# A transformer kernel's opening: ACT loads its table before it issues token tile 1, and the first key products run on tile 0 alone

## The chip, the cores and the metric

The kernel runs on one core of a Trainium2 chip. A core has five engines that run side by side, each through its own list of instructions in order: PE (TensorE: matrix products and transposes), DVE (VectorE), ACT (ScalarE), POOL (GpSimd) and SP (SyncE, which here only issues DMA transfers). They wait for each other through semaphores. The metric is the device time of one execution in microseconds (us), as a median of several runs.

## The reference

Two layers on 2048 tokens of width 1024; each layer is a windowed attention and a feed-forward part, both behind a layer norm and with a residual.

```python
def _A_ref(x, wqkv, wo):          # H = 32 heads of 32, window W = 8, dilation 2
    qkv = (x @ wqkv).reshape(B, S, 3, H, Dh) ...
    idx = pos[:, None] - (jnp.arange(W) * dil)[None, :]     # 8 earlier positions, every second one
    ...
    logits = jnp.where(mask, einsum("bhsd,bhswd->bhsw", q, kg) * scale, -1e9)
    o = einsum("bhsw,bhswd->bhsd", softmax(logits), vg)
    return o... @ wo
def _B_ref(x, w1, b1, w2, b2):    # F = 3584
    h = relu(x @ w1 + b1); return (h * h) @ w2 + b2
x = A_x
for _ in range(2):
    x = x + _A_ref(_layernorm(x), A_wqkv, A_wo)
    x = x + _B_ref(_layernorm(x), B_w1, B_b1, B_w2, B_b2)
```

Inputs and weights are bf16.

## The kernel before, in words

The 2048 tokens are cut into four blocks of 512 per layer, eight units of work (u = 0 to 7) in all. A unit goes through the stages SA (load four token tiles of 128, layer norm, transpose them to a tile xnT with the width of 1024 on the partitions), the projections (`projection`, lines 448 to 491: keys, queries, values, eight chunks of 128 columns each, PE accumulates over eight k-steps of 128, then ACT copies the result out of PSUM), S2 (window products on DVE, softmax, values), SW (output projection) and SF_up and SF_down (feed-forward).

The code doesn't issue the instructions as it runs. Every stage adds operations to a planner (`_Plan`), with an engine, an assumed duration, and the buffers that it reads and writes. `schedule` then plays the plan through with these assumed durations and puts each engine's operations in order by due time. PE's main work (`main=True`) keeps the order in which it was added; each main operation stands behind the one before. `issue_behind(a, b)` says that b may be issued only after a. Two instructions that write the same tile or share a buffer are put in an order by semaphores, whichever was emitted first going first. So a change in the opening can reorder what DVE, ACT and SP do later.

The opening is the function `first_projections` with SA(0):

- `SA` (line 428 on) loads four token tiles x0 to x3. x0, x2 and x3 go out through SP's queue, x1 through ACT's (`load_x`, line 413). Behind x0, SP issues four pieces of the key weights (two k-steps of 128 rows each), x2, x3, then four pieces of the query weights (`w_qkv`, line 347). ACT then loads its function table (line 436).
- PE first multiplies a tile of zeros (`spin`, line 743), eleven products of 512 columns whose result is not used.
- `layer_norm` (line 354 on) does, per tile: two halves of statistics on DVE (line 365), an aggregate on DVE (367), logarithm and exponential on ACT (368, 369), the normalisation on DVE (383), eight transposes on PE into one PSUM tile `pt` (398). For tiles 0 and 1 the transposed tile is copied to xnT in two halves: k-steps 0 to 3 by DVE (401), k-steps 4 to 7 by ACT (402). For tiles 2 and 3 DVE copies it whole (404). Lines 384 to 387 hold tile 0's normalisation back until tile 1's aggregate has been issued.
- Then come the key products of the first 256 tokens (tiles 0 and 1) for five of the eight chunks, step by step through all five chunks: tokens 0 to 127 with the first weight piece, tokens 128 to 255 with the first piece, then all 256 tokens with pieces two, three and four. Between the transposes of tile 0 and tile 1 stands one more product of zeros.
- After that: keys of chunks 5 to 7, tile 2's transposes, queries, tile 3's transposes, the second half of the tokens, and the values.

PSUM has six buffers that `pt`, the projections and most other products share (tag "mm"), so a product also waits until a buffer was copied out.

## Time and profile before

| | |
|---|---|
| median of three runs | 1238.55 us (1237.99 to 1238.65) |
| the profiled execution's own time | 1238.63 us |
| its span (first to last instruction) | 1236.9 us |
| PE busy | 1230.4 us, 99% |
| DVE, ACT, POOL busy | 67%, 45%, 14% |
| mean DMA rate | 206 GB/s |

The span is shorter than the execution's own time by what lies around the instructions. Engine rows in the profile give the start and the length of an instruction or of a run of equal ones; "[1.38 <-DVE xn L383]" says that the engine had been idle for 1.38 us and what ended that. A name with a q (SPq, ACTq) is the engine's sequencer, which issues DMAs and waits. `L398` is line 398 of the kernel before. The changed kernel is three lines shorter from line 387 on (its transposes are L395, its copies L398 and L399, its projections L472).

### The profile page before, as it was taken

The page shows a single profiled execution, that of the slowest core. Times are in us where ns is not written, and L with a number is a line of the kernel's source. Part 1 is how long each engine was busy: PE and PEld are TensorE (multiplying, and loading weights), DVE is VectorE, ACT ScalarE, POOL GpSimd, SP SyncE. Part 2 cuts the span into 40 slices and gives each one's busy share as a digit, 9 for nine tenths or more (in the row PEclk, how much of TensorE's full clock was granted, in tenths as well). Part 3 has the DMA queues.
Part 4 walks back from the last instruction along what each step waited for, and adds up shares of the span by engine and source line. Part 5 has one row for each costly group of instructions (what it writes and reads, how often), then busy time and mean ns, then how long its engine had stood idle before and what let it go on. Part 6 is the DMA issues. An engine that isn't in the chain of part 4 may idle for free.

```text
span 1236.9 us, 15608 instructions
## 1 busy us (share of the span) xinstructions
PE 1230.4 (99%) x5907; PEld 637.6 (52%) x5907; DVE 825.2 (67%) x1233; ACT 560.3 (45%) x1031; POOL 170.7 (14%) x200
## 2 busy tenths in 40 slices
PE   8999999999999999999999999999999999999998
PEld 7665444554455544555445554455544564444444
DVE  6899893698906979079770888609895199972001
ACT  5626920479104691048901578016770146612720
POOL 1351000040500100005050020000505011000000
PEclk9999999999999999999999999999999999999999
DMA  6858857688567985689755997548965596569441
GB/s 230 241 192 227 240 191 231 181 237 224 174 213 199 243 246 161 207 213 276 226 188 170 259 278 205 176 151 278 273 198 174 166 260 195 164 190 235 154 136 51
DMA packets 258277, 255.15 MB, mean 206 GB/s; under 512 B 70458, under 2 KB 221210, under 8 KB 258202
## 3 DMA queue, kind: packets, MB, share of 16 engines
q1 hardware_dynamic: 258058, 253.90, 69.5%
q8 instruction: 46, 0.75, 0.3%
q10 hardware_dynamic: 144, 0.26, 0.1%
q14 instruction: 29, 0.24, 0.1%
HBM read 209.98 MB, written 12.58 MB: 180 GB/s over the span
## 4 chain that ended last, share of the span: by engine, by line
PE 99%; DMA 0%; DVE 0%; issue 0%
PE py L715 31%; PE ph L690 31%; PE pq L475 27%; PE py L665 9%; PE lg L514 0%; DMA xt<-in_A_x_dram 0%; PE pt L398 0%; DVE stats L365 0%; PE junk L743 0%; DVE xo L725 0%; DVE xn L383 0%; DVE mv L367 0%; PE b1ps L329 0%
## 5 line engine op out<-in xcount | busy, mean ns | idle before, releaser
L715 PE MATMUL py<-wt,r2t 128*128 128x512 bf16 (+1 forms) x1820 | 388.3, 376 | 0.0
L690 PE MATMUL ph<-xnT,wt 128*128 128x512 bf16 x1792 | 388.1, 379 | 0.0
L475 PE MATMUL pq<-xnT,wt 128*128 128x512 bf16 (+2 forms) x1674 | 336.9, 362 | 0.0
L715 PEld LDWEIGHTS <-r2t 128*128 128x128 bf16 x1820 | 177.6, 98 | 209.4
L475 PEld LDWEIGHTS <-wt 128*128 128x128 bf16 x1674 | 229.9, 144 | 105.4 <-issue 3.4
L690 PEld LDWEIGHTS <-wt 128*128 128x128 bf16 x1792 | 174.9, 98 | 211.6
L484 ACT CAST kT<-pq 128x512 bf16<-128x512 f32 (+1 forms) x72 | 38.5, 540 | 352.7 <-PE pq L475 351.4
L693 ACT ACTIVATE r<-ph,b1T 128x512 bf16<-128x512 f32 x224 | 151.8, 678 | 51.0 <-PE ph L690 50.9
L502 DVE TENSOR_TENSOR P<-qT,kT 128x2048 bf16<-128x2048 bf16 x128 | 154.1, 1235 | 8.8 <-ACT qT L484 5.5
L615 DVE TENSOR_TENSOR pr<-pb,vT 128x2048 bf16<-128x2048 bf16 x128 | 153.3, 1234 | 7.6 <-DMA pb<-p 7.6
L695 ACT ACTIVATE r2t<-r 128x512 bf16<-128x512 bf16 x224 | 139.8, 629 | 5.7
L725 DVE TENSOR_TENSOR xo<-py,xm 128x512 bf16<-128x512 f32 (+1 forms) x33 | 22.3, 675 | 157.4 <-PE py L715 154.9
L618 DVE TENSOR_TENSOR pr<-pr 128x1024 bf16<-128x1024 bf16 (+1 forms) x256 | 126.7, 552 | 0.0
L519 DVE TENSOR_TENSOR P<-P 128x2048 bf16<-128x2048 bf16 x98 | 118.9, 1220 | 1.2
L665 PE MATMUL py<-wt,oT 128*128 128x512 bf16 x512 | 111.8, 379 | 0.0
L668 DVE TENSOR_TENSOR xm<-py,xt 128x512 f32<-128x512 f32 x64 | 43.0, 681 | 94.4 <-PE py L665 93.8
L491 POOL COPY khalo<-kT 128x7 bf16<-128x7 bf16 x64 | 20.2, 320 | 477.1 <-ACT kT L484 477.1
L491 POOL COPY vhalo<-vT 128x7 bf16<-128x7 bf16 x64 | 51.2, 809 | 243.7 <-ACT vT L484 243.2
L465 POOL COPY vT<-vhalo 128x7 bf16<-128x7 bf16 x32 | 67.0, 2143 | 125.5 <-DVE pr L615 125.3
L665 PEld LDWEIGHTS <-oT 128*128 128x128 bf16 x512 | 50.0, 98 | 60.2
L729 DVE TENSOR_TENSOR xm<-py,xm 128x512 f32<-128x512 f32 x32 | 21.5, 688 | 81.9 <-PE py L715 81.8
L368 ACT ACTIVATE lnv<-mv,eps 128x1 f32<-128x1 f32 x36 | 10.5, 292 | 95.0 <-DVE mv L367 95.0
(61 smaller groups left out, 547.6 us busy)
## 6 DMA issues: line engine op xcount, KB each, us to landing
wt<-in_B_w_dram SPq DMA_DIRECT2D x56, 1024.0 KB, 6.9
wt<-in_B_w_dram SPq DMA_DIRECT2D x64, 896.0 KB, 5.0
wt<-in_A_wqkv_dram SPq DMA_DIRECT2D x44, 1024.0 KB, 6.2
wt<-in_A_wo_dram SPq DMA_DIRECT2D x16, 1024.0 KB, 5.9
xt<-xs SPq DMA_DIRECT2D x32, 512.0 KB, 4.2
pb<-p SPq DMA_DIRECT2D x64, 128.0 KB, 4.5
xs<-xm SPq DMA_DIRECT2D x32, 256.0 KB, 3.4
xt<-in_A_x_dram SPq DMA_DIRECT2D x31, 256.0 KB, 4.0
```

Source lines behind the costliest of these rows:

```text
L465: add("POOL", 0.2, lambda: nc.gpsimd.tensor_copy(dst.t[:, 0:off], prev.t[:, c0, :]), r=[(prev, c0)], w=[(dst, 0)])
L475: nc.tensor.matmul(pq.t[:, a - t0:b - t0], w[:, kd % 4, c0:D:8], xnT.t[:, kd, a:b], start=first and kd == k0, stop=last and kd == k1 - 1, ...
L491: add("POOL", 0.2, lambda: nc.gpsimd.tensor_copy(halo.t[:, c0, :], dst.t[:, BLK:BLK + HALO]), r=[(dst, 2)], w=[(halo, c0)])
L502: st["dve"].append(add("DVE", 1.14, lambda: nc.vector.tensor_tensor(P.t[:], q.t[:, hb * HB:(hb + 1) * HB].rearrange("q (g t) -> q g t", g= ...
L519: self.state[u]["dve"].append(self.plan.add("DVE", 1.14, lambda: self.nc.vector.tensor_tensor(a.t[:], a.t[:], b.t[:], ALU.add), r=[b], w=[a]))
L615: dve.append(add("DVE", 1.14, lambda v=v, pr=pr: nc.vector.tensor_tensor(pr.t[:], pb.t[:], _win_ap(v.t, HALO + hb * HB, HB, groups=G), ALU ...
L618: dve.append(add("DVE", d, lambda pr=pr, k=k: nc.vector.tensor_tensor(pr.t[:, :, 0:k, :], pr.t[:, :, 0:k, :], pr.t[:, :, k:2 * k, :], ALU. ...
L665: nc.tensor.matmul(py.t[:], st["o", c].t[:, tl * 128:(tl + 1) * 128], st["wo"][db].t[:, c, :], start=(c == 0), stop=(c == self.NCH - 1))
L690: nc.tensor.matmul(ph.t[:], wt.t[:, kd, cc * 128:(cc + 1) * 128], xnT.t[:, kd, :], start=(kd == 0), stop=(kd == self.KD - 1))
L693: add("ACT", 0.58, lambda ph=ph, r=r, f=f: nc.scalar.activation(out=r.t[:], in_=ph.t[:], func=ACTF.Relu, bias=self.b1T[:, f:f + 1], scale= ...
L695: add("ACT", 0.54, lambda r=r, r2t=r2t: nc.scalar.activation(out=r2t.t[:], in_=r.t[:], func=ACTF.Square), r=[r], w=[r2t])
L715: nc.tensor.matmul(py.t[:], r2[kf].t[:, tl * 128:(tl + 1) * 128], wt.t[:, kf - k0, c0:c1], start=(kf == 0), stop=(kf == KF - 1))
```

## The change

Three places are touched. In `SA`, ACT's table load comes first and the issue of x1 behind it; before, it was the other way round. In `layer_norm`, tile 0's normalisation is no longer held behind tile 1's aggregate. In `first_projections`, the key products on tiles 0 and 1 are cut and ordered anew: three short products of zeros (128 columns) follow tile 0's transposes, then tile 0 alone goes through the first two weight pieces for five chunks (twenty products of 128 columns), then come tile 1's transposes, then tile 1 through the same two pieces (twenty more), and then both tiles together through pieces three and four. Before, the second piece was multiplied with both tiles at once. `spin` takes the number of columns, and its assumed duration follows from it.

```diff
-            aggr = add("DVE", 0.12, lambda: nc.vector.bn_aggr(...), r=[stats], w=[mv])
+            add("DVE", 0.12, lambda: nc.vector.bn_aggr(...), r=[stats], w=[mv])
...
-            norm = add("DVE", 0.45, lambda: nc.vector.tensor_scalar(out=xn.t[:], ...), r=[xt, mv, rstd], w=[xn])
-            if tl == 1:
-                plan.issue_behind(aggr, self.norm0)
-            self.norm0 = norm
+            add("DVE", 0.45, lambda: nc.vector.tensor_scalar(out=xn.t[:], ...), r=[xt, mv, rstd], w=[xn])
...
-            self.plan.issue_behind(x1, table)
+            self.plan.issue_behind(table, x1)
...
-    def spin(self, n):
+    def spin(self, n, cols=BLK):
...
-            add("PE", 0.427 if n > 4 else 0.3, lambda: nc.tensor.matmul(self.junk.t[:], self.zeros.t[:, 0:128], self.zeros.t[:], start=True, stop=True),
+            add("PE", cols * 8.3e-4, lambda: nc.tensor.matmul(self.junk.t[:, :cols], self.zeros.t[:, 0:128], self.zeros.t[:, :cols], start=True, stop=True),
                 r=[self.zeros], w=[self.junk], main=True)
...
-        for n, norm in ((11, norms[0]), (1, norms[1])):
-            self.spin(n)
-            norm()
+        self.spin(11)
+        norms[0]()
+        self.spin(3, 128)
...
-        early = first("wk", [(0, 128, 0, 2), (128, HB, 0, 2)] + pairs[1:])
-        for _ in range(5):
+        early = first("wk", [(t, t + 128, k, k + 2) for t in (0, 128) for k in (0, 2)] + pairs[2:])
+        for i in range(6):
+            if i == 2:
+                norms[1]()
             for p in early:
                 next(p, None)
```

In a step `(a, b, k0, k1)`, a to b are the tokens and k0 to k1 the k-steps.

More of the change, by code (lines that the diff above doesn't have):

```diff
@@ L366, in layer_norm @@
                     r=[(xt, h)], w=[(stats, h)])
-            aggr = add("DVE", 0.12, lambda: nc.vector.bn_aggr(out=mv.t[:], in_=stats.t[:].rearrange("p (n f) -> p n f", n=2)), r=[stats], w=[mv])
+            add("DVE", 0.12, lambda: nc.vector.bn_aggr(out=mv.t[:], in_=stats.t[:].rearrange("p (n f) -> p n f", n=2)), r=[stats], w=[mv])
             add("ACT", 0.2, lambda: nc.scalar.activation(out=lnv.t[:], in_=mv.t[:, 1:2], func=ACTF.Ln, bias=self.eps[:], scale=1.0), r=[mv], w=[lnv])
@@ L382, in layer_norm @@
         if pe_transpose:
-            norm = add("DVE", 0.45, lambda: nc.vector.tensor_scalar(out=xn.t[:], in0=src(), scalar1=mv.t[:, 0:1], scalar2=rstd.t[:],
+            add("DVE", 0.45, lambda: nc.vector.tensor_scalar(out=xn.t[:], in0=src(), scalar1=mv.t[:, 0:1], scalar2=rstd.t[:],
                                                             op0=ALU.subtract, op1=ALU.mult), r=[xt, mv, rstd], w=[xn])
-            if tl == 1:
-                plan.issue_behind(aggr, self.norm0)
-            self.norm0 = norm
         else:
```

## The prediction

> **What bounds the kernel now.** I read the page's head and chain first, then PE's waits, then the order of time of the first 28 us.

> The page, its head and the shares of the chain that ended last:

> ```profile
> span 1236.9 us, 15608 instructions
> PE 1230.4 (99%) x5907; PEld 637.6 (52%) x5907; DVE 825.2 (67%) x1233; ACT 560.3 (45%) x1031; POOL 170.7 (14%) x200
> PE 99%; DMA 0%; DVE 0%; issue 0%
> ```

> PE's waits over the whole span (who waited for whom; us, times, longest):

> ```profile
> PE junk L743 <- DVE zeros L741: 1.7, 1, 1.7
> PE pt L398 <- DVE xn L383: 1.4, 1, 1.4
> ```

> PE is the bound and waits only twice, both in the opening. After 7.99 us it never waits again, so whatever moves the opening moves the end one for one, and new PE idle time is added in full. The change lies in the opening alone; here it is in order of time (start, us, engine, line):

> ```profile
> 0.81 0.39 ACTq L413 DMA_DIRECT2D xt<-in_A_x_dram  x1
> 0.81 0.41 SPq L413 DMA_DIRECT2D xt<-in_A_x_dram  x1
> 1.23 1.28 ACT L436 ACT_TABLE_LOAD   x1 [1.23 <-PEq L832]
> 1.73 4.88 PE L743 MATMUL junk<-zeros 128*128 128x512 bf16 x11 [1.73 <-DVE zeros L741]
> 4.73 1.88 DVE L365 BATCH_NORM_STATS2 stats<-xt 128x6 f32<-128x512 bf16 x3 [2.74 <-DMA xt<-in_A_x_dram]
> 6.75 0.29 ACT L368 ACTIVATE lnv<-mv,eps 128x1 f32<-128x1 f32 x1 [4.24 <-DVE mv L367]
> 7.31 0.21 DVE L367 BATCH_NORM_AGGREGATE mv<-stats 128x2 f32<-128x12 f32 x1
> 7.43 0.49 DVE L383 TENSOR_SCALAR xn<-xt,mv,rstd 128x1024 bf16<-128x1024 bf16 x1
> 7.99 1.03 PE L398 MATMUL pt<-ident,xn 128*128 128x128 bf16 x8 [1.38 <-DVE xn L383]
> 9.06 0.42 DVE L401 COPY xnT<-pt 128x512 bf16<-128x512 bf16 x1 [0.40 <-PE pt L398]
> 9.52 0.58 ACT L402 COPY xnT<-pt 128x512 bf16<-128x512 bf16 x1 [1.44 <-DVE xnT L401]
> 10.93 1.88 DVE L365 BATCH_NORM_STATS2 stats<-xt 128x6 f32<-128x512 bf16 x3 [0.16 <-DMA xt<-in_A_x_dram]
> 17.55 0.61 PE L398 MATMUL pt<-ident,xn 128*128 128x128 bf16 x8
> 21.43 1.06 ACT L375 ACTIVATE xn<-xt 128x1024 bf16<-128x1024 bf16 x1 [3.30 <-DMA xt<-in_A_x_dram]
> 22.48 1.79 ACT L484 CAST qT<-pq 128x256 bf16<-128x256 f32 x6
> ```

> Three things are to be seen. Tile 0's normalisation (7.43) stands behind tile 1's aggregate (7.31). Each tile's transposes are copied in two halves, DVE first and ACT behind it, and the first key products need DVE's half only. And PE starts slow: eight transposes take 1.03 us at 7.99 but 0.61 at 17.55, the spins 0.43 each. Taken singly, products of 128 columns start 0.107 us apart up to 10.84 and 0.06 apart from 10.91 on; the trace's clock record begins at 10.85. I call that the release.

> **The change part by part.** Times below are in this execution's span (its own time 1238.63 us, 1.73 above the span; the median shown is 1238.55).

> *The issue of tile 1.* Nothing here shows a DMA issue behind a table load. Bounds: the table doesn't hold ACT's queue of issues, tile 1 goes out at about 0.85 and both tiles land as now (4.71 and 4.52); or it holds it for its 1.28 us, to 2.1. Tile 0 then has the DMA engines alone: they move 390 to 400 GB/s from 3 us on, so without tile 1's 256 KB it lands up to 0.67 us earlier, at 4.04. Tile 1 then lands 3.7 us (its time now) to 4.4 after its issue, 5.8 to 6.5, which DVE needs at about 6.6: hidden. I take the first: ACT's sequencer has a semaphore record at 23.91 in the middle of a CAST that runs until 24.27, so it runs ahead of its engine. On SP, the third query piece instead of the second now waits for tile 1; with keys and tiles 2 and 3 queued until 11.57 that starves nothing.

> *Tile 0 without tile 1 in front.* Statistics 4.73 to 6.02, aggregate 0.03+0.21, Ln 0.03+0.29, Exp 0.03+0.20, normalisation 0.04+0.52, hand-over to PE 0.06: transposes at 7.44 instead of 7.99, **0.55 us gained**.

> *Copies.* In the order that the planner writes for the changed kernel, ACT's half of a tile is copied first and DVE's copy waits for it. Transposes 1.03 + 0.04 + ACT 0.58 + 0.04 + DVE 0.42 + 0.06 = 2.17: the first key products start at 9.61. The three short spins cover 0.32 us (3 x 0.107), so PE sits idle from 8.61 to 9.61. Tile 1's first statistics half, now on DVE ahead of this copy, ends at about 8.0 and is hidden by ACT's copy, until 9.1.

> *Twenty products on tile 0* (five chunks, pieces 0 and 1), 0.107 each while slow: 9.61 to 11.74. Meanwhile tile 1 is normalised behind tile 0's DVE copy (ends 9.55): statistics to 10.15, aggregate, Ln, Exp and normalisation as above, to 11.53. Transposes of tile 1 at 11.74 (11.59 if the clock is up by then).

> *Tile 1's copies are bare.* PE's next work after these transposes is tile 1's own products, so transposes, ACT copy, DVE copy and hand-over lie in a row: 2.17 us, of which PE works 0.85. Now, twenty products of tile 0 and a spin cover that. Slow, tile 1's products start at 13.91; fast (0.61 for 1.03), at 13.34. Tile 2's statistics stand ahead of that DVE copy and wait for a tile landing at 10.9: hidden by 1.9 us.

> *Twenty products on tile 1*: ten products of 256 columns (0.109 each) became twenty of 128 (0.0615 in the ten from 11.03 to 11.65): +0.14. Done at 13.34+1.23 = 14.57 fast, 13.91+2.13 = 16.04 slow. Today the same products are done at 12.75. So **+1.8 us with the release at 10.85**, +3.3 in the slow case, plus half of the time that PE still runs slowly after 16.04.

> *Behind the opening.* ACT now has the next block's square (L376, L377: 0.2 + 1.15 + 0.19) in front of the query copies; it starts when a tile lands at 21.40, and the first copy ends at about 24.35 instead of 22.84. PE needs that bank at 23.70 today. With PE 0.66 us or more late this costs nothing; were PE not late, it would stall here, so no case ends below +0.66. Exp of tile 3 moved behind five key copies, but its transposes (20.19 today) come more than 1.5 us after the normalisation that follows. The opening's later SP queue differs only in which of the waiting transfers goes first (query-half, transposed tiles): PE's reduces and products have 1.5 us or more in hand over what they wait for up to 51 us, and the bound of that part is 0 to +0.3.

> *When is the release?* It decides between 1.8 and more. The row: it came 2.87 us after PE's restart at 7.99, in unbroken work. But the 4.7 us of unbroken spins from 1.73 brought none, so it isn't a count from a restart. A grid of fixed stretches fits: the stretch that ends at 10.85 was busier than the two before it. That allows a length of 3.2 to 3.65 us; at 3.41 the three are 67%, 70% and 84% busy. In the changed kernel (tile 1 issued early) the stretch 7.44 to 10.85 has 1.17 + 1.24 = 71% and 10.85 to 14.26 has 61%, nearest to those without a release; 14.26 to 17.67 is full. So: release at about 17.7, and from 16.04 on half of 1.63 = 0.8 us more. **Sum: 3.3 + 0.8 = +4.1 us.** A count of 2.87 us of unbroken work would run from 9.61 to 12.48, in the middle of the slow transposes' end: +2.4.

> [...]

> **The rivals.**
> 1. *Issued early, release at 10.85 as now*: for it, 71% is little more than the 70% that failed; +1.8, 1240.4.
> 2. *Issued early, release by unbroken work at 12.5*: +2.4, 1241.0; the spins speak against it.
> 3. *The table holds the issue (ending not slower than a measurement can tell).* Tile 0 lands at 4.04, transposes at 6.77; spins and transposes fill 90% of the stretch 4.03 to 7.44 and it releases at 7.44. Then the chain alone counts: 6.77 + 4.15 to tile 1's transposes (7.44 to 11.59 above) + 1.75 for these, fast, with both copies (2.17 - 0.42) + 1.23 = 13.9, **+1.2, 1239.7**. It decides if tile 0 lands before about 4.2 (at 4.2 that stretch is 84% busy). The sequencer record speaks against the hold.
> 4. *The table holds, and no release before 17.7* (tile 0 after 4.2): products on tile 1 done at 15.4, half of 2.3 us slow behind: +3.8, 1242.3.
> 5. *Faster*: the copies run side by side after all and the whole of tile 0's gain is kept. It needs tile 1's bare 1.3 us covered, which no row offers, and the query copies' floor of +0.66 stands against it.

> **How the numbers follow.** Forecast (early issue, late release) 40%, rival 1 15%, 2 12%, 3 18%, 4 10%, 5 and anything unseen 5%. Predicted: 1238.55 + 4.1 = 1242.6 us. Stretch lengths up to 3.65 give releases up to 18.15 and +4.4, with 0.3 behind the opening 1243.3; the low end is rival 3 at its earliest, +1.0, 1239.5. A measurement of this kernel can tell about 0.2%, 2.5 us, from no change, so 1241.0 is the border: the forecast, rival 4 and half of 2 lie above (56, rounded 57%), rivals 1 and 3 and the other half below (40%), 3% is left for faster.

> **What would show it.** Right: transposes at about 7.4; PE idle of 1.0 us ahead of the first L475 and 1.3 ahead of tile 1's, both put down to DVE's copy; that copy waiting for ACT's; no PE wait behind 14 us; a clock record that begins at 17 to 18 us. The table held: ACT's issue at 2.1, first statistics at about 4.1. Wrong altogether: PE waits beyond 20 us, or DVE's copy starting right behind the transposes.

## The result and the profile after

The changed kernel takes **1241.15 us** (1239.75 to 1242.06) where the kernel before took 1238.53 us (1237.89 to 1239.64) on the same chips: a ratio of **1.0019, 95% interval 1.0011 to 1.0026**, 2.6 us slower. That is on the border of what a measurement here can tell from no change. The forecast was 1242.6 us, with a range from 1239.5 to 1243.3.

The profiled execution of the changed kernel took 1239.92 us with a span of 1238.2 us, 1.3 us more than the span of before. PE's waits over the whole span (us in total, times, longest):

```profile
PE pq L472 <- DVE xnT L398: 2.1, 2, 1.1
...
PE pt L395 <- DVE xn L383: 1.1, 2, 0.6
PE ph L687 <- ACT r L690: 0.3, 1, 0.3
```

Before, PE waited once behind its spins. Now it waits four times in the opening: twice for a normalised tile, twice (2.1 us in all) for DVE's half of a copy. A short wait for ACT far behind the opening is new, too. Here is the opening in order of time (start, us, engine, line), first ACT's rows, then DVE's, then PE's:

```profile
0.80 1.28 ACT L433 ACT_TABLE_LOAD   x1 [0.80 <-PEq L831]
0.83 0.40 ACTq L410 DMA_DIRECT2D xt<-in_A_x_dram  x1
...
7.80 0.58 ACT L399 COPY xnT<-pt 128x512 bf16<-128x512 bf16 x1 [1.31 <-PE pt L395]
...
8.42 0.43 DVE L398 COPY xnT<-pt 128x512 bf16<-128x512 bf16 x1 [0.74 <-ACT xnT L399]
...
12.17 0.42 DVE L398 COPY xnT<-pt 128x512 bf16<-128x512 bf16 x1
...
7.13 0.64 PE L395 MATMUL pt<-ident,xn 128*128 128x128 bf16 x8 [0.53 <-DVE xn L383]
...
8.90 1.40 PE L472 MATMUL pq<-xnT,wt 128*128 128x128 bf16 x20 [0.96 <-DVE xnT L398]
10.90 0.62 PE L395 MATMUL pt<-ident,xn 128*128 128x128 bf16 x8 [0.60 <-DVE xn L383]
12.65 0.54 PE L472 MATMUL pq<-xnT,wt 128*128 128x128 bf16 x6 [1.13 <-DVE xnT L398]
```

Tile 0's transposes come 0.86 us earlier than before (7.13 for 7.99). Then the row of ACT's copy, DVE's copy and hand-over stands bare twice: PE is idle for 0.96 us ahead of tile 0's products and for 1.13 us ahead of tile 1's, and in between for 0.60 us, until tile 1 is normalised. Tile 1's twenty products, 0.0615 us each, are done at 12.65 + 1.23 = 13.88 where before had the same work done at 12.75: +1.1. The wait for ACT's `r` adds 0.3; together 1.4, of which 1.3 is seen in the span.

This execution is one of the faster ones. Its clock came up as the transposes began (0.64 us for the eight, not 1.03), and the trace's clock record begins at 7.20. Of the 14 runs, those whose mean granted clock prints as 1.0 took 1239.75 to 1240.36 us, those with 0.998 or 0.999, which by that mean were clocked lower for some time after the first record, 1240.40 to 1242.06. No run of the second group was profiled, so when and how far is not shown. The mean is a rough witness in two ways. Time ahead of the first record counts as full speed: the profile of before prints 1.0 though its products of 128 columns start 0.107 us apart up to 10.84 and 0.06 apart from 10.91 on. And a little half speed at the very end, where PE no longer works, counts as well (before's last 0.6 us).

### The profile page after: what moved, and what is told of

Read it like the earlier page. It is cut to its first block, busy times and chain, and to the rows that moved or that the text cites. A ratio compares the mean times of both kernels' runs of the same rounds, so it can differ in the third digit from the quotient of the medians.

```text
span 1238.2 us, 15524 instructions
## 1 busy us (share of the span) xinstructions
PE 1224.0 (99%) x5808; PEld 637.6 (51%) x5919; DVE 825.3 (67%) x1233; ACT 560.8 (45%) x1031; POOL 171.3 (14%) x200
## 4 chain that ended last, share of the span: by engine, by line
PE 98%; DMA 1%; issue 1%; DVE 0%; ACT 0%; SPq 0%
PE py L712 31%; PE ph L687 30%; PE pq L472 27%; PE py L662 9%; DMA xnT<-xn 1%; PE lg L511 0%; DMA xt<-in_A_x_dram 0%; PE pt L395 0%; DVE stats L365 0%; ACT xnT L399 0%; ACT xn L375 0%; DVE xn L383 0%; DVE xnT L398 0%; ACT lnv L368 0%; ACT r L690 0%
## 5 line engine op out<-in xcount | busy, mean ns | idle before, releaser
L488 POOL COPY vhalo<-vT 128x7 bf16<-128x7 bf16 x64 | 54.1, 854 | 239.8 <-ACT vT L481 239.5
L368 ACT ACTIVATE lnv<-mv,eps 128x1 f32<-128x1 f32 x36 | 10.5, 291 | 97.9 <-DVE mv L367 97.9
```

Of the source, the lines that this page charges most:

```text
L488: add("POOL", 0.2, lambda: nc.gpsimd.tensor_copy(halo.t[:, c0, :], dst.t[:, BLK:BLK + HALO]), r=[(dst, 2)], w=[(halo, c0)])
```

## The experiments

Two theories were set against each other. **Idle theory**: the loss is PE standing bare behind each of the two transpositions, by the order in which the planner puts the copies. **Clock theory**: the loss is the half-speed stretch that this idle time brings. Differences are against the kernel before on the same chip, whose medians were 1238.24 (the first three and the table alone), 1238.67 (the changed kernel again, the hold alone, the table put back, the first version of all together), 1238.45 (the order of tile 1's copy on two kernels, the second version of all together) and 1238.58 us (the order of the query copies). The 95% interval of most of these ratios reaches about 0.0009 to either side, 1.1 us, so smaller differences between two kernels are read from the traces' waits and not from the medians. Line numbers in a run's rows are those of its own kernel.

### DVE's half first

```diff
-                add("DVE", 0.4, lambda: nc.vector.tensor_copy(dst(0, mid), ...), r=[pt], w=[lo])
-                add("ACT", 0.5, lambda: nc.scalar.copy(dst(mid), ...), r=[pt], w=[hi])
+                c0 = add("DVE", 0.4, lambda: nc.vector.tensor_copy(dst(0, mid), ...), r=[pt], w=[lo])
+                c1 = add("ACT", 0.5, lambda: nc.scalar.copy(dst(mid), ...), r=[pt], w=[hi])
+                plan.issue_behind(c0, c1)
```

> The changed kernel, with ACT's half of the copies of tiles 0 and 1 issued behind DVE's half. Copies theory (the loss is that PE waits for DVE's copies, each 0.62 us later because ACT's copy of 0.58 us stands in front of it): PE's idle time ahead of the first key products falls from 1.19 to about 0.5 us, ahead of tile 1's products from 1.35 to about 0.7, and the median falls by 1.2 us to about 1239.9. Clock theory (the loss is a later release of the PE clock): the idle time falls but the median stays within 0.4 us of 1241.15, or follows only where the clock record begins earlier.

Measured: 1239.51 us (1239.07 to 1241.12), +1.27, with a span of 1237.7 us. PE's waits for DVE's copies fell from 2.1 to 1.4 us, all of it at tile 0 (0.3 us left); tile 1's longest is as before:

```profile
PE pq L473 <- DVE xnT L398: 1.4, 2, 1.1
...
PE pq L473 <- ACT qT L482: 0.2, 1, 0.2
```

DVE's rows in order of time show why tile 1's copy is still late:

```profile
10.91 0.69 DVE L365 BATCH_NORM_STATS2 stats<-xt 128x6 f32<-128x512 bf16 x1 [0.66 <-DMA xt<-in_A_x_dram]
11.52 0.41 DVE L398 COPY xnT<-pt 128x512 bf16<-128x512 bf16 x1
```

DVE stands idle for 0.66 us until tile 2 lands, works on its statistics, and copies tile 1 only then: the planner had put these statistics in front of the copy. Tile 1's products come 0.67 us earlier (11.98 for 12.65), and 0.2 us of that is given back to a new wait for a query copy; another 0.2 us goes to the wait for ACT's `r`, which was 0.3 in the changed kernel.

### Tile 1's transposes one step earlier

```diff
-            if i == 2:
+            if i == 1:
                 norms[1]()
```

> The changed kernel with tile 1's transposes one step earlier: ahead of the second weight piece on tile 0 instead of behind it, so ten products of tile 0 (0.62 us) lie over tile 1's copies. Copies theory: PE's idle time ahead of tile 1's products falls from 1.35 to about 0.7 us and the median by 0.6 us, to about 1240.5. Clock theory: the same idle time in all lies in other places, and the median moves by less than 0.3 us.

Measured: 1239.55 us (1239.43 to 1240.03), +1.31, span 1237.7. Half of tile 0's products now cover tile 1's copies: PE has one wait for DVE's copy left (1.0 us, tile 0's) and the same new wait of 0.2 us for a query copy. Each of the two bare idles can be taken away by itself, and each time the span of the one profiled execution is 0.5 us shorter than that of the changed kernel. The medians alone don't show these gains: the changed kernel was not run on this chip, and its own loss was +2.6 in its first runs and +1.37 on another chip (below).

This profiled execution holds a half-speed stretch (9.02 to 12.43; tile 1's transposes take 1.04 us) and yet took 1239.44 us, and the five runs with a mean clock of 0.999 lie among the six with 1.0. So here a half-speed stretch costs nothing that the time shows. A reason that fits, not tested, is that PE would only have waited longer for the query copy.

### The idle filled with products that nobody uses

Nine short products of zeros behind tile 0's transposes instead of three, and ten behind tile 1's.

```diff
-        self.spin(3, 128)
+        self.spin(9, 128)
...
                 norms[1]()
+                self.fill(10)     # products of zeros, 128 columns, into a buffer of their own
```

> The changed kernel with more products of zeros: nine of 128 columns instead of three behind tile 0's transposes, and ten behind tile 1's, where PE is idle today. Clock theory: PE is busy enough everywhere, the clock is released at about 7 us in every execution, the spread of 2.3 us shrinks to under 1 us and the median falls to that of the fastest executions of the changed kernel, about 1240.0. Copies theory: the real products still start when DVE's copies end, so nothing is gained below 1239.9; if the clock plays no part in the spread, the median stays at 1241.1.

Measured: 1239.92 us, +1.68; ten of the eleven runs lie within 1239.77 to 1240.06 and one at 1241.0. The mean clock prints as 1.0 in all of them. The spread of 2.3 us is nearly gone, and the median is no lower than what the changed kernel takes at full clock: with the clock held up, the order of the copies still costs its 1.7 us. The small spread is what the clock theory expected, the floor of 1239.9 what the copies theory expected; the two had forecast nearly the same median, so the median does not part them. One thing weakens this as a test of the clock alone: the later wait for ACT's `r` is absent here as well.

### The changed kernel once more, beside three others

> The changed kernel once more, beside the kernels it is to be compared with. Both theories: 1241.0 +- 0.5 us, +2.6 against before. Idle theory (the loss is PE standing bare behind each of the two transpositions, 1.2 and 1.35 us): the runs whose record shows full clock throughout lie +1.2 to +1.9 above before, and that part stays in every run. Clock theory (the loss is the half-speed stretch that the idle brings in some executions): runs with full clock lie within 0.5 us of before, and only those with a mean clock below 1 lie above.

Measured: 1240.04 us (1239.46 to 1241.62), +1.37, ratio 1.0015 (1.0006 to 1.0023), below the 1241.0 +- 0.5 that both theories expected. The four lowest runs, all at full clock, stay 0.8 to 1.1 us above before's median, and the two other runs at full clock 1.6 and 2.3 us. The clock theory wanted them within 0.5 us: the fixed part is there, with a lower end than the idle theory's +1.2. Its profiled execution (1240.97, full clock from 7.44 on) has the same opening within 0.2 us and yet a span of 1239.2, 1.0 more. The waits, ACT's rows in order of time, and ACT's row of the kernel before show where:

```profile
PE ph L687 <- ACT r L690: 1.2, 1, 1.2
```

```profile
432.96 1.06 ACT L375 ACTIVATE xn<-xt 128x1024 bf16<-128x1024 f32 x1 [8.26 <-DMA xnT<-xn]
...
434.02 0.67 ACT L690 ACTIVATE r<-ph,b1T 128x512 bf16<-128x512 f32 x1
```

```profile
430.31 1.06 ACT L375 ACTIVATE xn<-xt 128x1024 bf16<-128x1024 f32 x1 [6.51 <-DMA xnT<-xn]
```

At 433 us a statistics pass of layer two, which waits for a transfer, stands on ACT ahead of the copies that free PE's buffers. Before, that pass starts at 430.31 and PE does not wait. In the two profiles of the changed kernel it starts at 431.92 and 432.96 and costs 0.3 and 1.2 us. So there is a third term that neither theory had: a place far behind the opening that changes from run to run.

### Single parts of the change

The hold alone taken from the kernel before (table and products as before):

```diff
-            if tl == 1:
-                plan.issue_behind(aggr, self.norm0)
```

> The kernel before with one part of the change alone: the statistics of tile 1 are no longer held behind tile 0's normalisation; table behind tile 1's issue, products in pairs of 256 as before. Idle theory: PE's order and the copies of both tiles are as before, so no bare idle of over 0.7 us behind the transposes; 1238.2 +- 0.5 us. If the hold itself was what kept tile 0's normalisation early, it comes 0.6 us later and the time is 1238.8 us or more. Clock theory: the same work in the same stretches, 1238.2 us.

Measured: 1240.94 us (1240.30 to 1242.83), +2.27. Both theories missed. (The edit takes away the hold of tile 0's normalisation behind tile 1's aggregate; the expectation names it the other way round.) Its PE waits:

```profile
PE py L713 <- DVE xm L727: 1.5, 2, 1.0
PE ph L688 <- DMA xnT<-xn: 1.4, 1, 1.4
PE pq L473 <- ACT qT L482: 0.6, 1, 0.6
```

The opening is fine: no wait for a copy, first key products at 9.36 us, where before has them at 10.09. The loss is 3.5 us of waits at 23, 115, 192 and 194 us. One order less in the opening, and the planner puts later parts in another order; around 104 us, for instance, SP issues a second token tile ahead of two transposes (104.26 against 107.38 and 108.99), where before it came between two (109.11, behind 106.33 and ahead of 110.08). Which of these orders makes which wait was not followed further.

The table alone ahead of tile 1's issue, on the kernel before:

```diff
-            self.plan.issue_behind(x1, table)
+            self.plan.issue_behind(table, x1)
```

> The kernel before with one edit: ACT's table load ahead of the issue of tile 1. Both theories: tile 0 lands about 0.3 us earlier (4.4), because ACT's issue now follows SP's by 0.02 us instead of leading it; tile 0's normalisation is still held behind tile 1's aggregate, so PE starts 0 to 0.1 us earlier and the median stays within 0.4 us of 1238.5. If the table order were what costs the changed kernel its time, it would show +1 us or more here.

Measured: 1241.08 us (1239.30 to 1242.19), +2.84, another miss, and above the +1 us that was set as the sign of the table's order being the cost. DVE's rows in order of time:

```profile
10.96 0.69 DVE L365 BATCH_NORM_STATS2 stats<-xt 128x6 f32<-128x512 bf16 x1 [1.64 <-DMA xt<-in_A_x_dram]
11.57 0.41 DVE L401 COPY xnT<-pt 128x512 bf16<-128x512 bf16 x1
```

Here too tile 1's copy stands behind statistics that wait for tile 2's landing, and PE waits 0.8 us for it. The profiled execution is the fastest of its runs; what puts the others 1.5 us above it is not shown.

The table put back behind the issue, in the changed kernel:

```diff
-            self.plan.issue_behind(table, x1)
+            self.plan.issue_behind(x1, table)
```

> The changed kernel with the table put back behind tile 1's issue. Idle theory: tile 0 lands at about 4.7 us again and its transposes come at 7.9 to 8.0 us instead of 7.13, while the two idles behind the transposes stay at 1.0 to 1.35 us each: 0.3 to 0.9 us above the changed kernel's full-clock runs, 1240.4 to 1241.0 us, median with the clock's share 1241.6. If the table's place only matters through the copies' order (as in the kernel with the table edit alone), the time is that of the changed kernel, 1241.1 us, or below it.

Measured: 1241.20 us (1240.09 to 1242.35), +2.53, and 1.16 above the changed kernel's median on the same chip; lowest run against lowest run it is 0.63, within the idle theory's 0.3 to 0.9. Tile 0's statistics start at 4.76 instead of 4.40 and 4.55, its transposes at 7.95 instead of 7.13 and 7.28. So within the change the table's place is a part that gains, though the same edit alone cost 2.84 us. Not all of the 0.82 us is the landing (0.36): here DVE also works on half of tile 1's statistics ahead of tile 0's aggregate, three halves in a row where the changed kernel has two:

```profile
4.76 1.88 DVE L365 BATCH_NORM_STATS2 stats<-xt 128x6 f32<-128x512 bf16 x3 [2.76 <-DMA xt<-in_A_x_dram]
```

PE's rows show the clock falling in mid-opening:

```profile
7.95 0.67 PE L395 MATMUL pt<-ident,xn 128*128 128x128 bf16 x8 [2.08 <-DVE xn L383]
...
11.84 1.06 PE L395 MATMUL pt<-ident,xn 128*128 128x128 bf16 x8
```

Tile 0's transposes are fast (0.67 us), tile 1's slow (1.06), and the clock record has half speed from 8.39 to 15.21. PE also waits 0.7 us at 117 us for a transposed tile, so this profile does not price the table's place by itself.

### The orders put back, one at a time

The statistics of tiles 2 and 3 behind DVE's copy of tile 1, on top of DVE's half first:

```diff
+                if pe_transpose and tl >= 2:
+                    plan.issue_behind(self.copy1, o)     # o: this half's statistics
...
-                c0 = add("DVE", 0.4, ...
+                c0 = self.copy1 = add("DVE", 0.4, ...
```

> The changed kernel with VectorE's half of the copies first, as measured, and one order more: the statistics of tiles 2 and 3 behind VectorE's copy of tile 1. Theory (that copy stands behind the first statistics of tile 2, which wait for its landing near 10.9 us): PE's bare idle ahead of tile 1's products falls from 1.27 to about 0.65 us, and the query copies are also planned earlier, so the wait for the query copy (0.2 us) goes: 1238.6 +- 0.3 us where the kernel with the copies alone took 1239.5. Rival (the idle is the copy's own latency behind the transposes): still 1.2 us of idle and 1239.5 us.

Measured: 1239.39 us (1239.07 to 1239.90), +0.94. The opening did as the theory said: from PE's last transpose of tile 1 to its first product the starts lie 0.74 us apart, not 1.27. But the time hardly moved, because another wait grew from 0.2 to 0.9 us (PE's waits, then ACT's rows in order of time):

```profile
PE pq L475 <- ACT qT L484: 0.9, 1, 0.9
```

```profile
23.20 1.15 ACT L379 ACTIVATE xn<-xt,nmean 128x1024 bf16<-128x1024 bf16 x1
...
24.34 1.45 ACT L484 CAST qT<-pq 128x256 bf16<-128x256 f32 x5
```

The next block's square stands on ACT ahead of the query copies, and it waits for a token tile that lands at its own time. This is the floor that the prediction priced at +0.66; the fastest run here is 0.62 us above before's median. The next edit takes it away:

```diff
+            if self.qcopy:                               # in layer_norm, next block's first ACT statistics
+                plan.issue_behind(self.qcopy, o)
+                self.qcopy = None
...
+        if (u, nm, c0, half) == (0, "wq", 4, 0):         # the copy of the fifth query chunk
+            self.qcopy = o
```

> The changed kernel with VectorE's copies first, the order edge of tile 1's copy (together measured at 1239.4 us, with a PE wait of 0.9 us for the query copy at 24 us), and the first five query copies of half 0 ahead of the next block's first ACT statistics. Theory (the query copy behind that square takes back what the opening gains): the wait of 0.9 us goes, 1238.3 to 1238.7 us, and the record shows no PE wait beyond 14 us. Rival (the time is set by the half-speed stretches and what follows, the query wait is only seen because PE came early): 1239.2 to 1239.6 us, the 0.9 us reappearing at a later wait or as clock.

Measured: **1238.25 us** (1238.05 to 1239.59), 0.33 below before, ratio 0.9999 (0.9990 to 1.0008). The query wait is gone, and against before on each chip 1.3 us came off. One wait beyond 14 us is left against the expectation, 0.6 us at 432 us for ACT's `r`, the place seen above; that execution took 1239.06. So the change with three orders fixed is as fast as the kernel before: what it lost came of the planner's order, at three places. All eleven runs print a mean clock of 1.0, so this run does not say how much the orders gave by themselves and how much by keeping the clock up.

The order of DVE's copy on the kernel with the table alone:

```diff
 (the table alone, as above)
+                if pe_transpose and tl >= 2:
+                    plan.issue_behind(self.copy1, o)
```

> The kernel before with the table ahead of tile 1's issue, as measured (1241.1 us), and the statistics of tiles 2 and 3 behind VectorE's copy of tile 1. Theory (the table edit lost by the planner's order of that copy, not by the queue): no PE idle behind tile 1's transposes, 1238.0 to 1239.2 us, within 0.5 us of before. Rival (the half-speed stretches are the whole loss, the long idle ahead of the first transposes stays): 1240.5 to 1241.2 us.

Measured: 1244.97 us (1243.47 to 1245.44, five runs), +6.5, the slowest of all and outside both expectations. The idle behind tile 1's transposes is gone, and in its place stand these waits of PE:

```profile
PE py L717 <- DVE xm L731: 2.5, 2, 2.0
...
PE pq L477 <- ACT qT L486: 1.5, 1, 1.5
```

The 2.5 us are lost at 194 and 196 us, for the same buffer as at 192 and 194 us in the kernel without the hold. One order mended, two others disturbed; the half-speed stretch from 7.98 to 11.39 comes on top.

### All of it together

On the changed kernel: DVE's half first, tile 1's transposes one step earlier, the query copies ahead of the next block's statistics, the first half of tile 1's statistics ahead of tile 0's normalisation (where DVE waits for ACT's logarithm and exponential), and 12 and 6 spins for 11 and 3. First without the order of tile 1's copy, then with it. The lines not shown yet (`aggr0` and `norm0` are tile 0's aggregate and normalisation):

```diff
-        self.spin(11)
+        self.spin(12)
...
-        self.spin(3, 128)
+        self.spin(6, 128)
...
+                if pe_transpose and tl == 1 and h == 0:
+                    plan.issue_behind(self.aggr0, o, self.norm0)
```

> The changed kernel with four edits that keep PE covered: VectorE's half of the copies first, tile 1's transposes one step earlier, the first half of tile 1's statistics ahead of tile 0's normalisation, query copies ahead of the next block's first ACT statistics, and 12 and 6 spins for 11 and 3. Idle theory: the two bare idles shrink from 1.2 + 1.35 us to some 0.5 + 0.5 us, and 0.2 us of the wait for the query copy goes: 1.5 to 1.9 us below the changed kernel's full-clock runs, 1237.6 to 1238.6 us, level with before or up to 0.6 us below it, with a spread under 1 us. Clock theory: the stretches are filled above 79%, so the clock stays up, but the order of copies is worth nothing by itself: as the filled kernel, 1239.9 us. Early landing alone (tile 0's transposes 0.86 us earlier than before) would give 1237.4 us if all of it reached the end.

Measured: 1238.79 us, +0.12. Seven runs at full clock lie within 1238.67 to 1238.82; the other four, at a mean clock of 0.998 or 0.999, within 1240.26 to 1240.96. That misses both expectations, 1237.6 to 1238.6 us with a spread under 1 us and 1239.9. That a stretch has to be 79% full for the clock to stay up is shown by no run: with the hold alone it stayed up behind 49% (1.68 us of PE work from 5.01 to 8.42). The profile, one of the seven, has one long wait for DVE's copy left (1.7 us ahead of tile 1's products, with the copy at 11.64 behind tile 2's statistics at 11.03) and none behind the opening. The two groups, 1.5 to 2.2 us apart, go with the mean clock; that the clock alone parts them is not shown, as none of the four was profiled.

> The kernel with the four edits that keep PE covered (1238.8 us, with one bare idle of 1.94 us left ahead of tile 1's products) and the same order edge. Theory: that idle falls to 0.3 us or less, 1237.1 to 1237.6 us in most runs, 1.0 to 1.5 us below before. Rival (the later schedule takes back what the opening gains, or the landing of tiles 2 and 3 is needed sooner): 1238.5 us or more, with PE waits beyond 20 us that the kernel with the four edits has not.

Measured: **1237.00 us** (1236.93 to 1237.12), ratio **0.9989 (0.9980 to 0.9998)**, 1.45 below before. PE's rows in order of time:

```profile
7.27 0.62 PE L402 MATMUL pt<-ident,xn 128*128 128x128 bf16 x8 [1.17 <-DVE xn L390]
...
8.41 0.79 PE L480 MATMUL pq<-xnT,wt 128*128 128x128 bf16 x10 [0.18 <-DVE xnT L405]
9.27 0.62 PE L402 MATMUL pt<-ident,xn 128*128 128x128 bf16 x8
9.72 3.50 PE L480 MATMUL pq<-xnT,wt 128*128 128x128 bf16 x43
```

From 8.41 us on PE does not wait again, the pass at 433 us starts at 427.58, and the mean clock prints as 1.0 in all eleven runs. The change's gain, tile 0's transposes 0.72 us earlier, is now kept. It is not the whole of the 1.45 us: PE is fast here from these transposes on (0.62 us), and in the profile of before its first transposes take 1.03 us and its products are slow until 10.85. The kernel before with its clock up early was not run, so the two shares stay open.

## Why the prediction was right, and where it was wrong

**Slower, inside the range, 1.45 us too high at the point.** The steps in turn:

- *The issue of tile 1.* Right: ACT's issue is at 0.83, beside the table load (0.80 to 2.08). That tile 0 lands as now was wrong to the good side: its statistics start at 4.40, 0.33 earlier, and the 0.55 us gained became 0.86.
- *Copies.* Right in order and in cause: DVE's copy starts at 8.42, put down to ACT's. From transposes to first products it was 8.90 - 7.13 = 1.77 us; the 2.17 was the slow clock's, and without its 0.42 it is 1.75.
- *Tile 1's copies are bare.* Right to the hundredth for the fast case: 12.65 - 10.90 = 1.75 us. But "hidden by 1.9 us" for tile 2's statistics held only for a late tile 1. With these transposes at 10.9, the statistics are the next thing late, as DVE's half first showed; in the changed kernel ACT's copy (11.55 to 12.13) just covers them.
- *Behind the opening.* The floor of the query copies was right: it costs the changed kernel nothing and stops every faster opening, by 0.2 to 0.9 us. The bound of 0 to +0.3 for the rest was looked up to 51 us only; the place at 433 us cost 0.3 and 1.2.
- *When is the release?* This step failed. It took the stretch that ended at 10.85 in one execution of before and laid the changed kernel over the same grid: release at 17.7, with the slow case's 3.3 for 1.8 and the 0.8 behind it. The length of a stretch, 3.41 us, one value out of the 3.2 to 3.65 that before allows, was an estimate; the half-speed stretches of three other kernels last 3.41 us. The phase is not fixed: the record starts at 7.20 and 7.44 in the two profiles of the changed kernel, at 4.52 to 6.75 in ten other kernels. So there is no clock term, only a spread of it: nothing that the mean clock shows in 11 of the changed kernel's 25 runs, and in the slowest some 2 us, the place at 433 us included. With an early release the sum is the chain alone, 13.88 - 12.75 = +1.1. That is rival 3's total, reached without its cause: the table held nothing. One figure on the way was off as well: the 70% for the stretch 4.03 to 7.44 counts the spins at 0.427 us each; the view of stretches has PE busy for 2.58 us there, 76%.

Of its own signs, the idles ahead of the products (0.96 and 1.13 us for 1.0 and 1.3), put down to DVE's copy, and that copy waiting for ACT's came true. The clock record (7.20 for 17 to 18) did not, and the sign for "wrong altogether", a PE wait beyond 20 us, did come, with 0.3 and 1.2 us at 433 us.

That the median lies in the range is in part luck. The forecast's +4.1 us holds 2.3 us for a late release that neither profile of the changed kernel shows. The measured +2.6 is 1.1 us of the chain, 0.3 us or more at 433 us, and a rest in runs of which none was profiled.

The result stands 0.15 us above the border at 1241.0 that was set for "slower", and on another chip the changed kernel's median was 1240.04: which side it falls on hangs on how many of its runs have a mean clock below 1 or lose time at 433 us.

What the prediction had not seen at all is how far single edits reach: the hold alone costs 2.27 us, mostly beyond 20 us, the table alone 2.84. That the whole change is not worse than its parts is a property of this one plan.

## What to carry to other kernels

Where a planner orders the work, an edit in the opening is a new order of all that follows: compare the order of each engine's instructions, look for one that waits for a landing ahead of one that releases PE, and fix those few places with an explicit order. A gain in an opening is kept only if the next engine on the path (here ACT's query copies, which took back 0.2 to 0.9 us) is moved along. Take a clock's phase from no single execution (here the records began at 4.52 to 10.85 us): price it as a spread, or keep PE's idle short (with the idle filled, all eleven runs print a mean clock of 1.0).

## What the runs showed of the hardware

```profile
3.79:7.20 3.41, 2.88 (x8) 0.83 (x7) 2.17 (x5) 0.50 (x2) 0.00 (x0) 1.00 0.96 354
7.20:10.61 3.41, 2.13 (x31) 1.92 (x31) 2.03 (x5) 1.09 (x3) 0.00 (x0) 1.00 1.04 397
```

```profile
4.52:7.93 3.41, 1.19 (x7) 0.37 (x6) 3.21 (x7) 0.97 (x4) 0.00 (x0) 1.00 1.02 381
7.93:11.34 3.41, 3.28 (x27) 2.86 (x28) 1.35 (x3) 1.19 (x3) 0.00 (x0) 0.50 1.05 399
```

The changed kernel is released behind 2.88 us (84%) and stays fast behind 2.13 (62%); the table alone falls behind 1.19 (35%) and is released again behind 3.28 (96%). Thirteen profiles of this case fit two shares. The slow clock was left behind 2.74 us (80%, the changed kernel's second profile, 4.03 to 7.44) at the least, and not behind 2.60 (76%, the table put back, 8.39 to 11.80) or 2.58 (76%, before, 4.03 to 7.44). The fast clock was lost behind 1.48 us (43%, tile 1's transposes earlier, 5.61 to 9.02) at the most, and kept behind 1.68 (49%, the hold alone, 5.01 to 8.42) at the least. It was lost in the opening of four kernels, behind stretches that were 32% to 43% busy (1.10, 1.19, 1.33 and 1.48 us).

**Tile 0's landing.** In eight profiles of kernels with the table first, ACT's issue began at 0.83 or 0.84 us and tile 0's statistics started at 4.40 to 4.60. In three of them (the changed kernel, the table alone, all together without the order of tile 1's copy) SP's issue stands at 0.81, 0.02 us ahead. Where ACT's issue began at 0.80 or 0.81, they started at 4.73 (before) and 4.76 (the table put back), but in the kernel without the hold at 4.42. That the order of two issues decides it is not shown: nothing was run for it alone.
